# Linear attention and a multiplicative FFN on one core: a bfloat16 lead in the Gram sums, tiled features for batch 0 and for the second query block, and a new order of steps

## The chip, the cores and the metric

One core of one Trainium2 chip runs the whole program. The time is that of one execution on the device, in microseconds (us); of several runs the median is taken. The engines are TensorE (PE for its products, PEld for its weight loads), VectorE (DVE), ScalarE (ACT), GpSimd (POOL), and SyncE (SP), which issues most of the DMAs. Each engine works through its own instructions in a fixed order and waits for others only where data or a buffer makes it.

## The reference

```python
def phi(x):                                  # S1, S2: (8, 32)
    a = np.einsum('rd,bhsd->bhsr', S1, x)
    b = np.einsum('rd,bhsd->bhsr', S2, x)
    return np.einsum('bhsi,bhsj->bhsij', a, b).reshape(*x.shape[:-1], r * r)
q_p, k_p = (phi(q), phi(k))                  # q, k, v: (4, 4, 1088, 32)
kv = np.einsum('bhsf,bhsd->bhfd', k_p, v)
z = np.sum(k_p, axis=2)
num = np.einsum('bhsf,bhfd->bhsd', q_p, kv)
den = np.einsum('bhsf,bhf->bhs', q_p, z)[..., None] + 1e-06
attn_out = num / den
x = attn_out.transpose(0, 2, 1, 3).reshape(4352, 128)
a = x @ w1                                   # (128, 1024)
b = x @ w2
out = ((a * b) @ w3) @ w_out                 # (1024, 1024), (1024, 128)
```

Inputs are float64 and are handed over as raw 64-bit words; the output is float32. The denominator can come near zero, so its path is computed with split numbers (a coarse part on a grid, and a rest) so that the products of the coarse parts are exact.

## The kernel before

The program is written as named steps (`@step("...")` in `make_steps`). A string `ORDER` lists them; the steps are issued in that order, and every engine's instructions, and the DMAs among themselves, are chained in it. Nothing reorders them afterwards. `SLOTS` says for every tile which buffer of its kind it takes, in the order of allocation: `b` are the eight PSUM banks, `l`, `m`, `s`, `x`, `raw` are SBUF buffers of several sizes (`x` holds k, v and q of a batch). `POOL` and `ACTS` name the steps that run on GpSimd and ScalarE instead of VectorE (`on(name)`). A step can wait because its inputs aren't there or because the buffer that it takes is still read.

**Per batch b, keys and values.** `k{b}.load` brings 1024 rows of each head, `k{b}.loadr` the last 64. `k{b}.max` takes the largest absolute value, `k{b}.g` makes the grid (k_g), `lead` rounds k to it (on ACT in two activations, on DVE or POOL in one operation), `rest` is k minus lead; both lie in one float32 tile `kk`. `k{b}.gram0` to `gram4` (L607) sum, for each of 9 chunks and 4 heads, lead^T·[lead, rest] and rest^T·k: one product with 64 columns and one with 32 for each chunk and head, all float32, which run as two passes each. `Gm, Gt, Ga, Gb, T0, T1, Ta, Tb, Ts, N0, N1, Na, Nb, Nr` (`k_end`) make out of the Gram matrix and of S1, S2 (steps `s.*`) the matrix that gives the denominator; its results go to RC and AR (and RS, Rh for batch 0). The features of k are made in `kv(b)`: `tr`/`kT` turn k (through PE for batches 0 and 1, by DVE from `kh` for 2 and 3), `ab` multiplies by S, `kp0`, `kp1` form the 64 features, `kv0` to `kv3`, `kvr` sum features times v, and `kvm/kzt/kz` (batch 0) or `kvc/kqt/kq` lay the result out as weights. For batch 0, `ab0`, `ab1` (L650) are full-height products with kT as weights, copied out by ACT (`abc`); for the other batches `ab` (L675) works in 64x32 tiles and DVE turns the result (`abt`, L693). The last 64 rows of two batches go together (`kr0`, `kr1`).

**Queries.** q of a batch arrives with rows spread over heads. Block 0 (`q0`, 512 columns, kind "A") and block 1 (`q1`, 512 columns, kind "L") of batch 0 are done by `q_part`; batches 1 to 3 come as one block of 1024 each (`q2`, `q4`, `q6`), and the four last pieces of 64 rows as `qr`; these by `q_wide`. The steps of a block: `tr` turns it, `max`, `l2`, `l1` (ACT) and `rm` split it, `A*` and `C*` are the products with S and with the denominator's matrix, `sm, st, sh, sl, sc` split the results, `al, p01, p2, p12, dn, de, rc` give the reciprocal of the denominator, `bs` scales, `phi` forms the features, `pt/pc` (through PE and ACT, in `q_part`) or `pT` (by DVE, in `q_wide`) turn them, `x` multiplies by kv, and `xT` brings the result to the tile that the FFN reads. In `q_wide` the products work in 32x32 or 64x32 tiles, 16 or 8 side by side. In block 0 the scaling comes after x: `xs` multiplies by rc (DVE, L1206), `xt` turns it back (PE), `xT` copies (ACT).

**FFN.** Groups g0 to g7 have 512 tokens each and gr 256. For each group and each c of 8: `a` (L1453) and `b` (L1463) are products of 128x512, `c` copies a to SBUF (ACT), `m` multiplies (DVE, L1469), and `o` (L1476) adds the product with w3o to the group's sum in a bank. w3o = w3·w_out is made in 8 folds `f0` to `f7` (L479), each after its part of w3 has been converted from 64-bit words (`w{n}.c`, `w{n}.m` on ACT, `w{n}.j` on DVE, `w{n}.a0/a1` on POOL) and turned (`f.t`, DVE, L473). `oT` turns the sum (DVE) and `st` stores it (four DMAs on SP). g0 and g1 need q0 and q1, g2 and g3 need q2, and so on. g0 and g1 have 32 products a and b together, all in front of the first results of q2 unless the order puts some behind.

**Start.** Until the first `a`, PE's gaps are filled by products of zeros (`warm*`, L222). `c.act` is a copy of one element on ACT, whose only effect is that the table of activation functions is loaded there.

Of the kernel before, what the change touches and what calls it, by code (L numbers as in the profile page):

```python
# [24 lines left out]
        "s": "q1 s_t2 s_hla ay_A s_bs s_al kvc", "x": "k v qh"}  # L25
# [4 lines left out]
        "012345670123467012641234670513062571430516723512603215302725010760415320623547260134572614"  # L30
        "251376342057632057360276302162517325463712456142074372642354632462347562257341657163405264"
        "527053627367057653067434706730710014071506016364160573405671056454165341346354154112642167"
        "12047635102",
    "k_g": "0101",
    "l": "0123456789abc01246537804912cba076412583907a28bc67503914273a02145c0872195b6a34c8",
    "m": 
        "0123456789abcdefghijklmnopqrstuv3402158ab67cjefmil3hts8vc9dunb075c3hbnarkg7t4j38bv16euil9m"
        "oqs2htpe8u7oldnmt0qbjrchon294v5agd69s80onpvektuf387gbpkemd04lgntehs409vqodv9rsquh28rsft321"
        "gkcr",
    "q_m": "011010",  # L40
    "raw": "01210120120120120",
    "s": "0123456712054631027564013",
    "x": "012100120221",
}

WARM = [16, 10, 6] + [4] * 2 + [2] * 8 + [1] * 16
# [8 lines left out]
    k0.Nf k0.Nh k0.Nl k0.kp1 k0.rest0 k1.kp1 k2.kp0 k2.kp1 k2.rest0 k3.kp0 k3.rest0 q0.p01 q0.p12 q0.p2  # L55
    q0.scy q1.p12 q1.phi q2.bs q2.p2 q2.phi0 q2.phi1 q4.al q4.bs q4.p01 q4.p12 q4.phi0 q4.phi1 q4.sc
    q6.al q6.phi0 q6.phi1 qr.al qr.p12 s.blk s.blkh s.low s.rest s.sum
""".split())

ACTS = set("k0.lead1 k1.lead0 k2.lead0 s.lead".split())  # L60
# [15 lines left out]
g0.2a g0.3a q1.al q1.p01 q1.scy g0.2b q1.p2 g0.2c g0.1ac g0.3c w3.load k1.Gb v2.zero w1.a0 g0.5a g0.1ab q2.tr g0.7a
warm23 g0.6a g0.5c s.RC g0.7c g0.2m g0.1bb g0.1ba warm9 q1.p12 g0.0aa k2.rest0 w1.a1 g0.6c k1.T0 k1.T1 k2.gram0
k2.gram1 k2.gram2 k2.gram3 k2.gram4 q1.dn kr1.abc q2.max q1.de k1.Ta q1.rc w2.c k1.Tb k1.Ts q1.bs q2.l2 g0.0ac g0.1bc
k1.ab k1.N0 w3.c g0.1am q1.phi k1.N1 g0.4b g0.4a g0.1bm k1.abt k2.Gm k1.Na q2.l1 w3.m k2.Gt q1.pt1 q1.pt0 k0.Nr s.AR
q1.pc0 q1.pc1 g0.4c g0.7b g0.5b k1.Nb k1.Nr k2.Ga k1.kp0 k2.Gb q1.x q2.rm q2.C0 w3.j q1.xT w2.m w3.a0 w3.a1 v1.zero  # L80
q1.restT g0.5m q2.C1 q2.A0 g0.7m g0.4m q2.At q2.Ct g0.0ab g0.0am q2.sm g1.4a v1.load v1.loadr w2.j q2.st g1.0a g1.7a
g0.0bb k1.kp1 g1.6a g0.0ba g0.6b w4.load kh2.load g1.5a g1.4c g1.7c g1.6c q2.sh q2.sl q2.sc k1.kv0 k1.kv2 k1.kv3
q2.p01 k2.T0 k2.T1 k2.Ta q2.al k1.kv1 g1.5c g0.0bc k1.kvr k0.kqt k2.Tb g0.0bm g0.6m q2.p2 k2.kT0 k1.kvc w4.c w2.a0
q2.p12 q2.dn q2.de w2.a1 q2.rc g1.4b w5.load g1.1a q2.bs w4.m g1.6b g1.7b w5.m g1.7m f0.t q2.phi0 k3.zero g1.1b g1.2a
g1.5b w5.c q2.phi1 k0.kq q2.load k3.load g1.4m g1.0c g1.1c g1.1m g1.2c g1.5m g1.2b k2.kT1 k1.kqt f0.m k1.kq q2.pT0
kr1.kp w6.load f0.o q2.pT1 q2.restT g1.3a g1.3b g1.3c k2.Ts w4.j g1.3m q4.tr q2.x k2.N0 k2.N1 g0.3b q2.xT0 q2.xT1 w6.c
w6.m w9.load g0.3m g2.0a g3.6a w5.j g3.1a q4.max g3.6c g2.0c w5.a0 g2.1a g3.4a g3.3a g2.5a g3.1c g2.1c q4.l2 w5.a1
g2.1b w6.j g1.6m f2.t g2.7a w9.c g3.3c f2.m g1.0b w9.m g2.7c k2.Na w9.j k2.Nb g2.3a k3.loadr w4.a0 g3.0a f2.o g3.4c
q4.l1 g2.5c g2.3c g2.5b k2.Nr g3.0c w4.a1 g1.2m k2.ab g1.0m k3.max q4.rm q4.C0 w8.load w6.a0 q4.C1 q4.A0 k2.abt g2.5m
f1.t q4.At q4.Ct w8.m g2.4a g2.2a k2.kp1 w9.a0 w9.a1 w6.a1 f1.m g3.1b g2.6a g2.4b g3.5a f1.o w8.c g2.6c f6.t q4.sm  # L90
g3.1m q3.load w7.load q4.st g2.1m q4.sh w8.j w7.m w7.c g2.2c f3.t w8.a0 kh3.load k2.kp0 g1.0o v2.loadr g1.1o f6.m
g2.6b w7.j g0.0o g0.1o g0.2o k3.g k3.lead0 f6.o f3.m w7.a0 w7.a1 w8.a1 k3.kT0 f4.t q4.sl g2.4c f3.o q4.sc q4.al g2.6m
g1.6o g0.6o g1.3o g3.5c g2.2b g2.2m g2.7b g3.3b g3.2a g3.2c v2.load w10.load g2.7m f5.t g2.4m q3.restT f4.m k3.rest0
w10.c f5.m g3.4b q4.p01 q4.p2 w10.m q4.p12 q4.dn w10.j q4.de q4.rc q4.bs qr.max k2.kv0 k2.kv3 k2.kv1 k2.kv2 k2.kvr
q4.phi0 k3.gram0 k3.gram1 k3.gram2 q6.tr q6.max f5.o k3.gram3 k3.gram4 f4.o k2.kvc k2.kqt g3.6b w10.a0 k3.kT1 g3.4m
k3.Gm g1.4o k2.kq q6.l2 qr.l2 w10.a1 f7.t g2.3b g1.5o g2.0b g1.2o v3.zero k3.Gt g3.6m k3.Ga g2.0m g2.3m qr.l1 f7.m
g0.3o g0.5o g0.4o f7.o q6.l1 g3.3m k3.Gb q4.pT0 warm12 k3.T0 k3.T1 q4.phi1 q4.pT1 q6.rm q4.x k3.Ta k3.Tb k3.N0 k3.Ts
k3.N1 warm17 g1.7o k3.Na q4.xT1 g5.2a q4.xT0 k3.ab g1.oT k3.Nr k3.Nb q6.C0 k3.abt q6.C1 q6.A0 q6.Ct g0.7o v3.loadr
v3.load g1.st g4.4a q6.At g4.4b g2.0o q6.sm q6.st k3.kp0 g0.oT q6.sh k3.kp1 q6.sl g4.4c g2.4o g4.6a g4.6b g5.2c g4.6c
# [23 lines left out]
def make_steps(ctx, tc, q, k, v, S1, S2, moe_w1, moe_w2, moe_w3, moe_w_out, out):  # L123
# [3 lines left out]
    r = S1.shape[0]  # L127
# [430 lines left out]
    def k_split(b):  # L558
# [1015 lines left out]
```

## Time and profile before

| what | us |
|---|---|
| runs of the kernel | 250.39, 250.38, 249.95; median 250.38 |
| the profiled execution: time / span of its instructions | 250.19 / 248.4 |
| first product of the FFN (a_ps) | 28.77 |
| q2.x, q4.x, q6.x begin | 65.55, 123.01, 158.07 |
| last product (gr.o) ends | 245.17 |
| PE / DVE / ACT / POOL busy | 243.9 / 159.7 / 97.1 / 78.7 |

All times within the profile are from the start of the span. The profile's parts are: busy time of each engine; the span in 40 slices (about 6.2 us each), where a digit is the busy share in tenths; the chain of work that ended last; the groups of instructions by line, with mean duration, and with the idle time of the engine ahead of them and what ended it; and, from the trace, the instructions of an engine in order of time (start, duration, line, operation, tiles, a count where equal ones follow on each other, and in brackets how long the engine had been idle and what released it). Matmuls overlap, so the time of a run of products is read from start to start, not from the sum of durations. A float32 product shows as two instructions. The granted clock is 1.00 in every stretch.

### The profile page before, as it was taken

How to read it: one execution, taken by the hardware profiler on the slowest of the kernel's cores; microseconds unless marked ns; L12 is line 12 of the kernel's file. 1: busy time of each engine (PE TensorE's matmuls, PEld its weight loads, DVE VectorE, ACT ScalarE, POOL GpSimd, SP SyncE). 2: the span in 40 equal slices, each digit the busy share in tenths (PEclk: the TensorE clock that was granted, in tenths of full speed). 3: DMA queues.
4: the chain of work that ended last, by engine and by line, in shares of the span. 5: the costliest groups of instructions: out<-in, count | busy, mean ns of one | idle time of the engine just before them, and what ended most of it. 6: DMA issues, size and time to landing. Idle time of an engine off the chain costs nothing.

```text
span 248.4 us, 5734 instructions
## 1 busy us (share of the span) xinstructions
PE 243.9 (98%) x2375; PEld 139.2 (56%) x2375; DVE 159.7 (64%) x337; ACT 97.1 (39%) x178; POOL 78.7 (32%) x104
## 2 busy tenths in 40 slices
PE   8999999999999999999999999999999999999996
PEld 6889756464645556485644454444444445564455
DVE  4988999989988898887969483504256315142410
ACT  4578978458488271153213103422023221411000
POOL 5446693709473639769030005000000000000000
DMA  6889824887799307503020000002000000001563
GB/s 190 246 214 278 262 62 124 213 190 227 173 226 236 83 7 219 118 3 92 3 42 3 0 4 0 3 1 42 3 0 0 0 3 0 0 0 22 89 101 66
DMA packets 31130, 22.01 MB, mean 89 GB/s; under 512 B 21248, under 2 KB 25600, under 8 KB 30976
## 3 DMA queue, kind: packets, MB, share of 16 engines
q1 hardware_dynamic: 30416, 21.05, 34.8%
q10 hardware_dynamic: 688, 0.59, 0.7%
q8 instruction: 19, 0.31, 0.6%
q14 instruction: 7, 0.06, 0.1%
HBM read 19.40 MB, written 2.23 MB: 87 GB/s over the span
## 4 chain that ended last, share of the span: by engine, by line
PE 88%; DMA 4%; SPq 2%; DVE 2%; issue 1%; POOL 1%; ACT 0%; POOLq 0%; DVEq 0%
PE b_ps L1463 24%; PE a_ps L1453 24%; PE ps_o L1476 22%; PE ps_w3o L479 6%; DMA k<-in_k_dram 4%; PE ps_x L1412 2%; PE ps_ac L1299 2%; PE ps_or L1483 1%; PE ps_g L607 1%; PE ps_kv L717 1%; SPq L395 1%; DVE k_m L181 1%; PE ps_ab L675 1%; PE idle_ps L222 1%; POOL kk L599 0%
## 5 line engine op out<-in xcount | busy, mean ns | idle before, releaser
L1469 DVE TENSOR_TENSOR ab<-ffa,b_ps 128x512 f32<-128x512 f32 (+1 forms) x74 | 44.8, 633 | 44.3 <-PE b_ps L1463 33.5
L1458 ACT COPY ffa<-a_ps 128x512 f32<-128x512 f32 (+1 forms) x74 | 38.7, 558 | 87.0 <-PE a_ps L1453 78.9
L1463 PE MATMUL b_ps<-xT,w 128*128 128x512 f32 (+1 forms) x148 | 67.2, 561 | 0.0
L1453 PE MATMUL a_ps<-xT,w 128*128 128x512 f32 (+1 forms) x148 | 66.5, 560 | 0.0
L1476 PE MATMUL ps_o<-ab,w3o 128*128 128x512 f32 x128 | 60.7, 594 | 0.0
L1453 PEld LDWEIGHTS a_ps<-xT,w 128*128 128x128 f32 x148 | 27.5, 190 | 30.8 <-issue 24.0
L1463 PEld LDWEIGHTS b_ps<-xT,w 128*128 128x128 f32 x148 | 27.1, 190 | 27.0 <-issue 20.8
L1476 PEld LDWEIGHTS ps_o<-ab,w3o 128*128 128x128 f32 x128 | 23.9, 190 | 25.3 <-issue 23.7
L443 POOL TENSOR_TENSOR w3c<-cv_c,cv_m 128x512 int32<-128x512 int32 x16 | 21.1, 1349 | 13.1 <-DVE cv_c L432 13.1
L1492 DVE STREAM_TRANSPOSE oT<-ps_o 128x512 f32<-128x512 f32 x8 | 5.7, 715 | 22.9 <-PE ps_o L1476 22.9
L479 PEld LDWEIGHTS ps_w3o<-wo,w3T 128*128 128x128 f32 x128 | 15.3, 192 | 2.9 <-issue 2.2
L1394 POOL TENSOR_TENSOR ph<-s_al,s_bs 128x1024 f32<-128x1024 f32 x6 | 11.7, 1954 | 12.0 <-DVE s_bs L1384 11.8
L479 PE MATMUL ps_w3o<-wo,w3T 128*128 128x128 f32 x128 | 15.4, 275 | 0.0
L625 POOL TENSOR_TENSOR kp<-kabt 128x1024 f32<-128x1024 f32 x4 | 8.2, 2062 | 16.6 <-DVE kabt L693 16.6
L230 ACT ACTIVATE cv_c<-raw 128x1024 f32<-128x1024 f32 x11 | 12.8, 1164 | 0.6 <-issue 0.6
L222 PE MATMUL idle_ps<-zeros 128*128 128x256 bf16 x72 | 12.0, 313 | 1.0 <-DVE zeros L194 1.0
L418 ACT ACTIVATE cv_m<-raw 128x1024 int32<-128x1024 uint32 x11 | 12.8, 1172 | 0.0
L473 DVE STREAM_TRANSPOSE w3T<-w3c 128x1024 f32<-128x1024 f32 x8 | 9.9, 1240 | 3.9 <-POOL w3c L443 2.8
L222 PEld LDWEIGHTS <-zeros 128*128 128x128 bf16 x72 | 7.8, 112 | 3.6 <-DVE zeros L194 1.0
L1365 POOL TENSOR_TENSOR s_pr<-s_pr 128x256 f32<-128x256 f32 (+1 forms) x2 | 1.1, 526 | 25.3 <-DVE s_pr L1361 25.3
L483 ACT COPY w3o<-ps_w3o 128x128 f32<-128x128 f32 x8 | 2.0, 267 | 17.5 <-PE ps_w3o L479 17.5
L1402 DVE STREAM_TRANSPOSE pT<-ph 128x1024 f32<-128x1024 f32 (+1 forms) x7 | 7.9, 1147 | 0.0
(245 smaller groups left out, 292.4 us busy)
## 6 DMA issues: line engine op xcount, KB each, us to landing
raw<-in_moe_w_dram SPq DMA_DIRECT2D x32, 256.0 KB, 5.0
qh<-in_q_dram SPq DMA_DIRECT2D x4, 544.0 KB, 6.2
out_dram<-oT SPq DMA_DIRECT2D x33, 64.0 KB, 2.0
raw<-in_moe_w_dram SPq DMA_DIRECT2D x4, 512.0 KB, 7.6
k<-in_k_dram SPq DMA_DIRECT2D x3, 512.0 KB, 6.4
v<-in_v_dram SPq DMA_DIRECT2D x2, 512.0 KB, 4.4
raw<-in_moe_w_out_dram SPq DMA_DIRECT2D x1, 1024.0 KB, 8.7
kh<-in_k_dram SPq DMA_DIRECT2D x8, 128.0 KB, 2.5
```

The costliest lines, as they stand in the source:

```text
L222: pe.matmul(t, zeros, bview(zeros, [[0, 2], [1, 128]]), start=True, stop=True)
L230: act.activation(dst, hi.bitcast(F32), ACT.Prelu, scale=2.0 ** -112, alpha=-2.0 ** 32)
L418: act.mul(x["m"], words(0).bitcast(U32), 2.0 ** -29)
L443: pool.tensor_tensor(d, c, m, ALU.add)
L473: dve.transpose(w3T[ko].rearrange("p s (i r) -> p s i r", r=32), bview(w3c[ko], [[32, NC], [256, 4], [1, 32]]))
L479: pe.matmul(t["o"], w3T[ko][:, c], wo[:, c], start=c == 0, stop=c == NC - 1)
L1394: on(nm(f"phi{u}")).tensor_mul(x, bview(s["al"][:, u * g], [[r, g], [1, r], [0, r]]), bview(s["bs"][:, u * g], [[r, g], [0, r], [1, r]]))
L1453: pe.matmul(x["a"][:, :w], w_of(0, c), xT[g][:, c0:c0 + w], start=True, stop=True)
L1458: act.copy(x["s"][:, :w], x["a"][:, :w])
L1463: pe.matmul(x["b"][:, :w], w_of(1, c), xT[g][:, c0:c0 + w], start=True, stop=True)
L1469: dve.tensor_mul(ab_sb[g, c][:, c0:c0 + w], x["s"][:, :w], x["b"][:, :w])
L1476: pe.matmul(o_ps[g], w3o[:, c], ab_sb[g, c], start=c == 0, stop=c == NC - 1)
```

## The change

The Gram sums of batches 1 to 3: the lead is written in bfloat16 (into the first half of kk), the products lead^T·lead are bfloat16 with 32 columns (`gramH`); then `plus` replaces k by k + lead, and rest^T·(k + lead) is summed in float32 with 32 columns (`gram0`, `gram1`); `Gb` adds half of that sum and half of its transpose (`Gy`). Batch 0 keeps the float32 products, but has three grids of its own: heads 0 and 1, heads 2 and 3, and the last rows of all. Batch 0's features go the way of batch 1's (tiles, `abt`). Block 1 of the queries goes through `q_wide` (512 columns) instead of `q_part`. In block 0, x is now computed with kz as weights, so that it comes out turned; the reciprocal is spread by an ACT copy (`rb`), turned by PE (`rT`) and multiplied in by DVE (`xT`). `POOL` and `ACTS` name other steps, the warm products have other counts, `SLOTS` and `ORDER` are new from end to end.

```diff
-    k0.Nf k0.Nh k0.Nl k0.kp1 k0.rest0 k1.kp1 k2.kp0 k2.kp1 k2.rest0 k3.kp0 k3.rest0 q0.p01 q0.p12 q0.p2
-    q0.scy q1.p12 q1.phi q2.bs q2.p2 q2.phi0 q2.phi1 q4.al q4.bs q4.p01 q4.p12 q4.phi0 q4.phi1 q4.sc
-    q6.al q6.phi0 q6.phi1 qr.al qr.p12 s.blk s.blkh s.low s.rest s.sum
+    k0.Nf k0.Nh k0.Nl k0.Nr k0.Ts k0.rest0 k0.rest1 k0.rest2 k1.Nr k1.kp0 k1.kp1 k1.rest0 k2.kp0
+    k2.rest0 k3.Nr k3.Ts k3.kp0 k3.kp1 k3.plus k3.rest0 q0.al q0.p01 q0.p12 q0.p2 q0.phi1 q0.sca q0.scy
+    q1.al q1.p01 q1.p12 q1.p2 q1.phi0 q2.al q2.bs q2.p12 q2.p2 q2.phi0 q2.phi1 q2.sc q4.bs q4.p01
+    q4.phi0 q4.phi1 q4.sc q6.al q6.phi0 q6.sc qr.al qr.p01 qr.p12 qr.p2 qr.phi0 s.AR s.KS s.Pp s.blk
+    s.blkh s.low s.sum
-ACTS = set("k0.lead1 k1.lead0 k2.lead0 s.lead".split())
+ACTS = set("k0.lead0 k0.lead1 k0.lead2 k1.lead0 k2.lead0".split())
 ORDER
-s.load c.mask k0.zero c.zeros k0.load0 k0.loadr c.ident warm24 warm22 warm18 warm0 k0.load1 q0.load warm21 c.act
-s.words s.four k0.max0 s.pair k0.max1 k0.max2 k2.zero k0.tr1 k0.g s.lead warm3 warm1 warm7 s.low k0.lead0 k0.lead1
+c.zeros k0.zero k0.load0 c.mask s.load k0.load1 s.words c.ident k0.max0 warm0 warm1 k0.tr1 k0.g0 k0.loadr s.pair
+k0.max1 s.four s.lead s.low k0.lead0 q0.load k0.g1 k0.tr0 s.sum k0.max2 k0.lead1 s.rest k1.zero kr0.load k0.g2 warm2
+s.T s.tc s.P k0.rest0 warm3 s.R k0.kT1 k1.loadr q1.tr kr0.tr k0.rest1 k0.lead2 k1.load s.zero s.Pc warm4 k0.gram0
...
+k2.rest0 q3.restT q6.tr w6.a1 g2.0m f1.m g2.1c k2.ab q4.C0 q4.A0 f3.t q4.C1 f1.o k3.gramH k3.kT0 k3.plus q4.At k3.gram0
...
+qr.p01 g3.2o g2.4o qr.p2 qr.p12 qr.dn q6.bs c.act q6.phi0 q6.phi1 g4.4b g3.4o g2.7o g4.3m q6.pT0 q6.pT1 g3.5o q6.x
...
+gr.7c gr.2o1 g5.1o g5.7o gr.0o0 gr.2o0 g5.oT gr.5o1 gr.6b gr.7m g6.st gr.6m gr.1o0 gr.3o0 gr.4o0 g7.st gr.6o0 gr.6o1
+gr.7o1 gr.5o0 gr.7o0 gr.oT0 gr.oT1 g5.st gr.st1 gr.st0
```
```diff
 def k_split(b):
+        parts = ((0, 2, 0, NJ), (2, H, 0, NJ), (0, H, NJ, NK))
...
+        def lead_of(x):
+            t = bview(x, [[1, H * NK * D // 2]]).bitcast(BF16)
+            return t.rearrange("p (h j d) -> p h j d", h=H, j=NK)
...
+        @step(f"k{b}.plus")
+        def _():
+            on(f"k{b}.plus").tensor_add(k_sb[b], k_sb[b], k_lead[b])
 def gram(b):
+        if b > 0:
+            @step(f"k{b}.gramH")
+            def _():
+                a["g"] = ps("kvz", [128, 2 * D], "ps_g")
+                for j in range(NK):
+                    for h in range(H):
+                        prod(h, k_lead[b][:, h, j], k_lead[b][:, h, j], a["g"][:, :D], j == 0, j == NK - 1)
+            for u in range(2):
+                @step(f"k{b}.gram{u}")
+                def _(u=u):
+                    for j in range(*((0, 5), (5, NK))[u]):
+                        for h in range(H):
+                            prod(h, kk[b][:, 1, h, j], k_sb[b][:, h, j], a["g"][:, D:], False, j == NK - 1)
+            return
 def k_end(b):
+            dve.scalar_tensor_tensor(a["Gb"], a["g"][:, D:], 0.5, a["Gb"], ALU.mult, ALU.add)
+            dve.scalar_tensor_tensor(a["Gb"], a["Gy"], 0.5, a["Gb"], ALU.mult, ALU.add)
 def q_part (block 0)
+                    s["x", u] = o = ps("h", [128, 256], "ps_xt")
+                    for p in range(2):
+                        pe.matmul(o[64 * p:64 * (p + 1)], kz[b][:, 64 * p:64 * (p + 1)], s["pT"][:, p, part],
+                                  start=True, stop=True)
...
+                    dve.tensor_mul(x_dst()[:, part], x_dst()[:, part], s["rT", u])
     for g in range(8):
-        if g < 2:
-            q_part(g, b, half * 512, 512, "AL"[g])
+        if g < 1:
+            q_part(g, b, half * 512, 512, "A")
```

325 lines of the change are left out of this document (154 added, 171 removed).

## The prediction

> **What bounds the kernel now.** I read the busy line and the slices first, then the busy time in four stretches, then the rows where the stretches meet.
>
> ```profile
> PE 243.9 (98%) x2375; PEld 139.2 (56%) x2375; DVE 159.7 (64%) x337; ACT 97.1 (39%) x178; POOL 78.7 (32%) x104
> PE   8999999999999999999999999999999999999996
> DVE  4988999989988898887969483504256315142410
> ```
> ```profile
> 0.00:28.77 28.77, 26.69 (x586) 23.36 (x587) 23.00 (x70) 20.18 (x40) 14.46 (x52) 1.00 0.79 240
> 28.77:65.55 36.78, 36.78 (x449) 20.45 (x448) 35.15 (x86) 24.86 (x39) 22.98 (x22) 1.00 0.68 170
> 65.55:123.00 57.45, 57.45 (x600) 34.50 (x604) 50.26 (x76) 27.15 (x44) 33.90 (x25) 1.00 0.48 114
> 123.00:245.20 122.20, 122.20 (x748) 60.52 (x748) 50.97 (x108) 24.92 (x56) 7.39 (x6) 1.00 0.12 18
> ```
>
> Columns of the second view: stretch, then busy us of PE, PEld, DVE, ACT, POOL, then clock, DMA share, GB/s. PE looks full everywhere, but until 28.77 (first FFN product, a_ps) it is partly padded by `warm` products. From 28.77 on it does real work without a gap. DVE is nearly as full until 65.55 (35.15 of 36.78), then lighter. So there are two joints at which both run out together; they are where the tiled block of 1024 queries gets its output product `x`:
>
> ```profile
> 63.27 2.33 DVE L1402 STREAM_TRANSPOSE pT<-ph 128x1024 f32<-128x1024 f32 x2
> 65.55 0.81 PE L1412 MATMUL ps_x<-pT,kq 32*32 32x256 f32 x32
> ...
> 119.65 2.37 DVE L1402 STREAM_TRANSPOSE pT<-ph 128x1024 f32<-128x1024 f32 x2
> ```
> ```profile
> 31.16 0.86 PE b_ps L1463 x2
> ...
> 37.00 1.70 PE ps_g L607 x85
> ...
> 123.01 1.38 PE ps_x L1412 x58
> ...
> 241.60 3.57 PE ps_or L1483 x32
> ```
>
> DVE ends the pT of q2 at 65.60 and PE's q2.x starts at 65.55 (it takes the first half early): call this **A**. DVE ends q4's at 122.0 and q4.x starts at 123.0: **B**. Before A, PE has used up 30 of the 32 full FFN products that exist for the first two groups, so it can't run ahead of DVE there. From B to the last product (245.17) only PE counts. I therefore forecast A, then PE's work from A to B, then from B to the end; the rest (250.19 of the profiled execution less 245.17 = 5.0 us) stays: the stores of the last groups take about 0.5 us each on SP, and the 16 of g4, g6, g7, g5 now queue ahead of gr.st1 for 8 us, but their first data is there some 8 us before the end. The median of the runs, 250.38, is 0.19 above the profiled execution. From no change a measurement of this kernel tells about 0.2% (0.5 us).
>
> **Up to A: DVE.** Both kernels issue exactly 155 DVE instructions up to the second pT of q2. Added, by rows of the same shape: two k.plus (128x1152, 1.35 each) 2.7; pT of the second block 1.16; two more w.j conversions 1.38; two kabt transposes 0.78; six 128x128 transposes for q1's A and C (0.31 each) 1.86; two G_y and two more G_b operations 0.84; four small S steps from ACT and POOL 0.7. Sum 9.4. Removed: k0's lead and rest 0.66 + 0.78, k1's rest 1.35 (to POOL), one kT 0.69, one phi half 0.68, q1's and q2's corrections 0.86, three al 0.99, q0's sca 0.30, p01, p2 and p12 1.31, the P2 steps 0.64, KS and AR 0.9, half an ab 0.38. Sum 9.5. Net -0.1.
>
> Waits: `c.act` moves to the far end, so ACT's table load no longer runs beside the first transfers but behind them, with the first real activation:
>
> ```profile
> 1.74 1.28 ACT L215 ACT_TABLE_LOAD   x1 [1.74 <-issue]
> ...
> 3.71 0.26 ACT L230 ACTIVATE sk_c<-s_raw 8x64 f32<-8x64 f32 x1 [0.49 <-DMA s_raw<-in_S_dram]
> ```
>
> sk_c then starts at about 5.0. Behind it on ACT stand k0's two leads, and DVE's s.pair waits: with max0 and g0 done at 4.4, DVE idles till 5.2: +0.8. The Gram of k0 starts at about 9.7 (8.32 now), but DVE gets to it only at 11.75, behind two transposes, two q maxima and k1.max, so nothing more comes of that. DVE's wait of 0.76 for k2 at 24.46 goes: k2.load is issued some 2 us earlier and its maximum is asked for later. That is -0.76. The scaling of block 0 by a transposed reciprocal has as many DVE, PE and ACT steps as now; its chain (rc, copy, transpose, multiply) is as long as xs, xt, xT, and x now runs beside it: 0.
>
> POOL gets 13.6 us more before A (37.4 now): 2.64 for k1.rest0, 1.75 for k0's rests, 1.27 for half a phi, 1.27 for q2.sc, 0.62 for kpr, the rest small. Where both engines read at once the trace shows stretches:
>
> ```profile
> 36.20 0.99 DVE L1124 SCALAR_TENSOR_TENSOR s_rc<-s_d 128x16 f32<-128x16 f32 x1
> ...
> 94.04 1.90 DVE L587 TENSOR_TENSOR k_g<-k_m,grid 128x2 f32<-128x2 f32 x1
> ```
> ```profile
> 93.52 2.41 POOL L625 TENSOR_TENSOR kp<-kabt 128x1024 f32<-128x1024 f32 x1
> ```
>
> s_rc takes 0.17 elsewhere, k_g 0.15. Summed, DVE lost about 1.6 us in 37.4 us of POOL before A, and 5.1 in 33.9 between A and B: 0.04 to 0.15 per us of POOL. For 13.6 us that is 0.6 to 2.0; I take 0.8, the rate of the same stretch. A moves by -0.1 + 0.8 - 0.76 + 0.8 = **+0.7**, to 66.3.
>
> PE does not set A: its work from 28.77 loses q1's four-by-two transposes (0.88), a kqt (0.22), three warm products (0.33), 0.26 of x and 0.55 of Gram (below), and gets 1.5 FFN products more (at 0.858): 35.8 instead of 36.8 us. It can start at about 28.1, since DVE's work ahead of the first xT is 0.6 more and its waits some 0.4 more, but the new order begins with half products that need half of xT. So PE could be at A by 63.9. What PE saves before its first FFN product (C of q1, about 1.1; x of q0, about 1.4) only replaces warm-up time: 0.
>
> **A to B: PE.** Counting the products in both orders: 44.5 full FFN products instead of 43 (+1.29), k3's N0 and N1 now before B (+0.24), two warm products fewer (-0.2), and k3's Gram. That is 144 passes in 1.70 us now; its first 8 wide passes take 0.14 us, the next 7 narrow ones 0.06, so 17 and 8.5 ns a pass. Afterwards 72 narrow passes stay (0.6) and 36 bf16 products of 32 columns with their own weight load come: at least the narrow pass (8.5 ns, 0.31), at most the bf16 products of L976 (four in 0.10, 0.90). I take 15 ns, 0.54: the Gram saves 0.55, bounds 0.2 and 0.8. Sum **+0.8**.
> The Trainium skill, TensorEngine Tiling (Array Packing), section Instruction Overhead, speaks against a fourfold gain from bf16: a product carries some 60 cycles of its own, so that few columns cost as much as 60. By it the bf16 product costs what the narrow pass costs, the Gram saves 0.8, and the sum would be 248.6; by the trace's bounds it is 248.6 to 249.2.
> DVE's work grows by 4.0 there (a q.rm 1.1, a kp 1.13, T steps 0.85, a kT 0.62, p12 0.6, al 0.35, G_y 0.35, less two w.j): 54.3 of 58.2 us. It fits if its idle 7.2 us shrink to 4.
>
> **B to the end: PE.** 124 full products instead of 127 and N gone: **-2.8**. The new order puts 39 products between q4.x and q6.x (33 now), so q6 has more cover; 17 before qr.x cover its short chain.
>
> Sum: 250.19 + 0.7 + 0.8 - 2.8 = **248.9**.
>
> **Rivals.**
> *PE alone bounds* (DVE's waits close up, POOL does not disturb): A at 63.9, so -1.65 + 0.8 - 2.8 gives 246.5. For it: PE is full from 28.77. Against it: DVE's sum up to A is unchanged. 0.14.
> *POOL holds DVE up before A*: at 0.15 per us and with POOL's own steps stretched once (p01 of q0 took 1.78, the same shape 0.73 elsewhere), A moves by 0.7 + 1.2 + 0.4, and the time is 250.5, no change. 0.15. The Trainium skill, SBUF — State Buffer, section Who interferes with whom, gives this as a lock: a DVE instruction with two SBUF inputs and a GpSimd instruction exclude each other, for the whole instruction. The trace agrees at k_g: it ends at 95.94, the POOL kp at 95.93.
> *DVE becomes the bound between A and B, and the change is slower*: its idle time there is not slack but waits for POOL's w3c, PE's b and the k3 chain (k3.max, lead, then rest0 and plus on POOL, 2.64 each, before PE's k3.gram0 that stands in the middle of PE's queue). If all 7.2 us of waiting stay, A to B takes 61.5 instead of 58.2: 252.2. It decides from about 2.1 us kept beyond the forecast's 4. For it: DVE is 88% busy there now and gets 8% more. Against it: PE's FFN work lies in wait on every other step. 0.25.
> *The change does not do what it says*: the bf16 Gram costs as much as the f32 one. Only k3's share lies on the path: +0.55, 249.4, inside the forecast's band.
>
> **How the numbers follow.** Forecast 248.9 (247.7 to 249.7) 0.46; PE alone 246.5 0.14; POOL's hold 250.5 0.15, a third of it over 250.9; DVE bound 252.2 0.25, a fifth of it under 250.9. Faster 0.62 (the first two and a little of the third), same 0.13, slower 0.25. The range reaches from 246.2 to 252.0 and leaves out the upper half of the last case and a little of the second.
>
> **What would show it.** Right: sk_c at about 5.0 behind the table load; the Gram of k2 and k3 in 0.9 to 1.5 us; q2.x at 66.3 with DVE's pT just ahead; q4.x about 58 us later; last product at 243.9. Wrong: q2.x before 65 (PE or a shorter DVE queue bounds), or PE gaps before k3.gram0 or q4.x with DVE busy there.

## The result: 6 % slower, and the profile after

The changed kernel takes 265.17 us (median of 4 runs, 264.07 to 267.8), the kernel before 250.22 beside it: 1.061 times, 95% interval 1.053 to 1.070. Ratios, here and below, leave out executions that took over 1.5 % longer than the fastest of their kernel; medians keep them. The forecast was 248.9 with a range up to 252.0. The profiled execution of after took 265.82, with a span of 264.0. Its busy line and slices:

```profile
PE 249.4 (94%) x2374; PEld 135.3 (51%) x2374; DVE 170.0 (64%) x335; ACT 96.7 (37%) x179; POOL 100.6 (38%) x126
PE   8969798898899997999999999999999999999995
DVE  3959899899999998999557913571363013461212
PEclk9977979999799999999999999999999999999999
```

PE was full from its first FFN product in the kernel before; now it has gaps in the first sixteen of the 40 slices, and among these the granted clock falls too. DVE is busy for 170.0 us instead of 159.7, with two instructions fewer. Where the time went is told by three stretches, up to joint A (q2.x begins), from A to joint B (q4.x begins) and from B to the last product. First the kernel before, then after; columns: stretch, busy us (and instructions) of PE, PEld, DVE, ACT, POOL, clock, DMA share, GB/s:

```profile
0.00:65.55 65.55, 63.47 (x1034) 43.81 (x1034) 58.14 (x155) 45.03 (x78) 37.44 (x73) 1.00 0.73 200
65.55:122.94 57.39, 57.39 (x591) 34.45 (x590) 50.20 (x76) 27.15 (x44) 33.90 (x25) 1.00 0.48 114
122.94:245.20 122.26, 122.26 (x750) 60.58 (x748) 51.03 (x108) 24.92 (x56) 7.39 (x6) 1.00 0.12 18
```
```profile
0.00:79.94 79.94, 70.30 (x1080) 42.24 (x1080) 69.38 (x154) 47.84 (x81) 54.86 (x91) 0.91 0.68 178
79.94:141.31 61.37, 59.57 (x570) 34.22 (x573) 52.62 (x86) 24.39 (x42) 33.81 (x25) 1.00 0.39 89
141.31:260.90 119.59, 119.50 (x738) 58.80 (x736) 48.05 (x97) 24.22 (x55) 11.97 (x11) 1.00 0.10 18
```

A is 14.4 us late, A to B 4.0 longer, B to the end 2.7 shorter. Up to A, DVE issues 154 instructions instead of 155, yet is busy for 11.2 us more, and idle for 10.6 instead of 7.4. POOL is busy for 17.4 more. The same instructions have become longer. Seven of them, from DVE's timeline of after (start, duration, engine, line, operation):

```profile
22.45 3.20 DVE L663 TENSOR_TENSOR kp<-kabt 128x1024 f32<-128x1024 f32 x1
31.96 1.24 DVE L1149 SCALAR_TENSOR_TENSOR s_rc<-s_d 128x16 f32<-128x16 f32 x1
35.58 0.89 DVE L602 TENSOR_TENSOR k_g<-k_m,grid 128x2 f32<-128x2 f32 x1
39.53 2.30 DVE L170 SCALAR_TENSOR_TENSOR s_t<-s_g,ay_A 128x256 f32<-128x256 f32 x1
55.22 2.31 DVE L1301 SCALAR_TENSOR_TENSOR q<-q,qT 128x1024 f32<-128x1024 bf16 x1
61.69 2.09 DVE L170 SCALAR_TENSOR_TENSOR s_t<-s_g,ay_A 128x512 f32<-128x512 f32 x1
65.60 1.12 DVE L839 SCALAR_TENSOR_TENSOR G_b<-G_y,G_b 128x32 f32<-128x32 f32 x1
```

Undisturbed, they take some 1.2, 0.16, 0.12, 0.37, 1.2, 0.65 and 0.18 us, by the shortest instruction of the same operation and shape in the traces. What GpSimd did meanwhile, from its timeline:

```profile
21.17 3.40 POOL L617 TENSOR_TENSOR kk<-k,kk 128x1152 f32<-128x1152 f32 x1 [0.31 <-DMA raw<-in_moe_w_dram]
...
39.18 2.38 POOL L617 TENSOR_TENSOR kk<-k,kk 128x1152 f32<-128x1152 f32 x1 [1.47 <-ACT kk L178]
...
55.18 3.52 POOL L445 TENSOR_TENSOR w3c<-cv_c,cv_m 128x512 int32<-128x512 int32 x2
...
61.28 1.96 POOL L663 TENSOR_TENSOR kp<-kabt 128x1024 f32<-128x1024 f32 x1
```

The kp of 22.45 starts while k1's rest runs, which ends at 24.57, and ends 1.1 us behind it, about its own undisturbed time; s_t of 39.53 ends at 41.83, k2's rest at 41.56. So two steps on GpSimd hold up two DVE instructions by 2 us each. k1's rest was moved there by the change; k2's was there in the kernel before too (33.27 to 35.91), but beside transposes, reductions and a product that reads PSUM, and held up none of them. Counted over the stretch up to A, 18 DVE instructions that read SBUF alone and run beside GpSimd are over 0.1 us longer than their shortest, by 14.2 us together; in the kernel before there are 7, by 2.0 us.

The waits on DVE ahead of A: 2.25 us at 17.42 for q0.C0, which stands behind kr1.tr on PE; 0.86 for sk_c; 1.58 for GpSimd, 1.42 of it before the sums that read its p12. The first of these I had not foreseen. PE's row and DVE's, from their timelines:

```profile
16.03 0.33 PE L782 MATMUL ps_krt<-ident,kr 128*128 128x128 f32 x1 [1.94 <-issue]
...
17.42 0.29 DVE L1037 TENSOR_REDUCE s_ga<-ps_ac 128x16 f32<-128x128 f32 x1 [2.25 <-PE ps_ac L992]
```

"issue" says that PE waited 1.94 us for nothing that the profile shows.

### The profile page after: what moved, and what is told of

It reads as the page before. It is cut to its first block, busy times and chain, and to the rows that moved or that the text cites. A ratio compares the mean times of both kernels' runs of the same rounds, so it can differ in the third digit from the quotient of the medians.

```text
span 264.0 us, 5765 instructions
## 1 busy us (share of the span) xinstructions
PE 249.4 (94%) x2374; PEld 135.3 (51%) x2374; DVE 170.0 (64%) x335; ACT 96.7 (37%) x179; POOL 100.6 (38%) x126
## 4 chain that ended last, share of the span: by engine, by line
PE 76%; DVE 17%; issue 3%; POOL 2%; ACT 1%; DVEq 0%; POOLq 0%
PE b_ps L1487 20%; PE ps_o L1500 20%; PE a_ps L1477 18%; PE ps_w3o L481 4%; PE idle_ps L224 3%; DVE kp L663 2%; PE ps_x L1436 2%; DVE s_t L170 2%; DVE ab L1493 1%; PE ps_or L1507 1%; PE ps_ac L1323 1%; DVE q L1301 1%; PE ps_kv L732 1%; PE ps_ab L693 1%; DVE k_m L183 1%
## 5 line engine op out<-in xcount | busy, mean ns | idle before, releaser
L1493 DVE TENSOR_TENSOR ab<-ffa,b_ps 128x512 f32<-128x512 f32 (+1 forms) x74 | 45.4, 631 | 52.1 <-PE b_ps L1487 41.6
L1477 PE MATMUL a_ps<-xT,w 128*128 128x512 f32 (+1 forms) x148 | 67.4, 576 | 0.1
L1477 PEld LDWEIGHTS a_ps<-xT,w 128*128 128x128 f32 x148 | 28.3, 196 | 30.1 <-issue 22.6
L1487 PEld LDWEIGHTS b_ps<-xT,w 128*128 128x128 f32 x148 | 27.3, 191 | 28.5 <-issue 23.1
L445 POOL TENSOR_TENSOR w3c<-cv_c,cv_m 128x512 int32<-128x512 int32 x16 | 23.4, 1487 | 11.4 <-PE ps_o L1500 5.8
L1418 POOL TENSOR_TENSOR ph<-s_al,s_bs 128x1024 f32<-128x1024 f32 (+1 forms) x7 | 13.8, 1979 | 19.7 <-DVE s_bs L1408 19.6
L224 PE MATMUL idle_ps<-zeros 128*128 128x256 bf16 x67 | 12.8, 345 | 1.1 <-DVE zeros L196 1.0
L1447 ACT COPY xT<-ps_x 128x256 f32<-128x256 f32 (+2 forms) x20 | 5.1, 343 | 15.9 <-PE ps_x L1436 8.1
L1375 POOL TENSOR_TENSOR s_al<-s_hl 128x256 f32<-128x256 f32 (+2 forms) x4 | 4.2, 1055 | 17.4 <-DVE s_hl L1370 17.2
L663 POOL TENSOR_TENSOR kp<-kabt 128x1024 f32<-128x1024 f32 x5 | 10.2, 2042 | 1.6 <-DVE kabt L711 1.6
L1426 DVE STREAM_TRANSPOSE pT<-ph 128x1024 f32<-128x1024 f32 (+1 forms) x8 | 9.1, 1161 | 1.4 <-POOL ph L1418 1.4
```

What stands on the lines that cost most here:

```text
L224: pe.matmul(t, zeros, bview(zeros, [[0, 2], [1, 128]]), start=True, stop=True)
L445: pool.tensor_tensor(d, c, m, ALU.add)
L663: eng.tensor_mul(dst, bview(av, [list(av.ap[1]), list(av.ap[2]), [0, r]]), bview(bv, [list(bv.ap[1]), [0, r], list(bv.ap[2])]))
L1418: on(nm(f"phi{u}")).tensor_mul(x, bview(s["al"][:, u * g], [[r, g], [1, r], [0, r]]), bview(s["bs"][:, u * g], [[r, g], [0, r], [1, r]]))
L1477: pe.matmul(x["a"][:, :w], w_of(0, c), xT[g][:, c0:c0 + w], start=True, stop=True)
L1487: pe.matmul(x["b"][:, :w], w_of(1, c), xT[g][:, c0:c0 + w], start=True, stop=True)
```

## Experiments

Thirteen kernels in five steps. Where a step is moved, the slot letters that it takes move with it; that part of the diffs is left out. In the table, A is the start of q2.x in the profiled execution, DVE its busy time up to there, idle the rest; the ratio is to the kernel before as it ran beside each (medians 249.9 to 250.63), with its 95% interval.

| kernel | A | DVE busy | idle | median us | ratio |
|---|---|---|---|---|---|
| before | 65.55 | 58.14 | 7.41 | 250.22 | 1 |
| after | 79.94 | 69.38 | 10.56 | 265.17 | 1.061 (1.053 to 1.070) |
| tr_late | 77.64 | 68.89 | 8.75 | 263.89 | 1.051 (1.045 to 1.056) |
| warm_fill | 79.67 | 69.33 | 10.34 | 264.02 | 1.054 (1.051 to 1.058) |
| rest_dve | 76.89 | 67.81 | 9.08 | 262.53 | 1.045 (1.040 to 1.051) |
| before_pool | 73.05 | 54.35 | 18.70 | 257.40 | 1.026 (1.021 to 1.030) |
| pool_old | 83.23 | 69.80 | 13.43 | 266.93 | 1.068 (1.065 to 1.070) |
| pool_old_tr | 81.27 | 69.32 | 11.95 | 266.86 | 1.069 (1.061 to 1.077) |
| gram_alone | 71.41 | 62.22 | 9.19 | 258.72 | 1.033 (1.028 to 1.038) |
| mix | 76.48 | 67.63 | 8.85 | 262.75 | 1.051 (1.043 to 1.058) |
| mix_gram_old | 79.48 | 63.47 | 16.01 | 267.26 | 1.070 (1.065 to 1.076) |
| dummy_pool | 69.91 | 63.40 | 6.51 | 254.64 | 1.017 (1.015 to 1.019) |
| w0_late | 82.13 | 68.78 | 13.35 | 264.58 | 1.056 (1.052 to 1.059) |
| rest_cut | 77.01 | 65.26 | 11.75 | 263.12 | 1.052 (1.049 to 1.055) |

The variants of the changed kernel scatter by 0.4 to 2 % from run to run, the kernel before and dummy_pool by 0.6 % or less; differences of 1 us between two of them are not read as differences of time, only their traces are.

### Step one: four single edits

**tr_late**
```diff
-... q1.l1 warm5 k0.T1 kr1.tr v0.load s.KS q0.C0 ... k0.Na k0.Nh k1.tr1 ...
+... q1.l1 warm5 k0.T1 v0.load s.KS q0.C0 ... k0.Na k0.Nh kr1.tr k1.tr1 ...
```


> The changed kernel with one step moved: the transposes of k's last rows (kr1.tr) stand on PE after k0's ab instead of ahead of q0's C. Theory P (GpSimd's added work stretches VectorE's instructions: summed, 11.2 of the 14.4 us that joint A came later): only the 2.25 us wait of VectorE behind that step goes, so q2.x moves from 79.9 to 77 to 78 and the time from 265.2 to 262 to 263.5. Rival C (TensorE's empty 2 us and the fall of the granted clock behind it cost most): the clock stays at 1.00 from 16 to 24, and 6 us or more come back: below 260.

A comes 2.3 us earlier, within theory P's bounds: the wait at q0.C0 shrinks from 2.25 to 0.58 us, and little else changes. The clock stays at 1.00 from 16 to 24, and the median is 1.3 us lower (263.89; P said 262 to 263.5), not rival C's 5 or more. But the moved step is hardly what did it. PE's stop at this place lasted 0.47 us here instead of 1.94 (what it is comes in step three). In w0_late (step four) kr1.tr stands as in the changed kernel, the stop lasts 0.51 us, and DVE waits as little. First tr_late, then w0_late:

```profile
15.85 0.29 DVE L1037 TENSOR_REDUCE s_ga<-ps_ac 128x16 f32<-128x128 f32 x1 [0.58 <-PE ps_ac L992]
```
```profile
15.84 0.29 DVE L1037 TENSOR_REDUCE s_ga<-ps_ac 128x16 f32<-128x128 f32 x1 [0.62 <-PE ps_ac L992]
```

**warm_fill**
```diff
-WARM = [3, 16, 14, 2, 6, 1, 2, 1, 5, 11, 6]
+WARM = [3, 16, 14, 2, 6, 18, 2, 1, 5, 11, 6]
-... q1.l1 warm5 k0.T1 kr1.tr ...
+... q1.l1 k0.T1 warm5 kr1.tr ...
```


> The changed kernel with 17 more warm products on PE just ahead of kr1.tr, where it waits 2 us for its DMA: the wait of VectorE stays as it is, only TensorE is kept busy. Expected in both theories: the granted clock no longer falls to 0.50 between 17 and 23. Theory P: VectorE sets the pace there, so at most 1 us comes back: 264 to 265.5. Rival C (the lower clock itself costs): 3 us or more come back: below 262.

From 17 to 23 the clock is 1.00, in after 0.50. A moves by 0.3 us. It is not a clean test of the price: in this run the clock fell to 0.50 earlier, from 10.8 to 14.2, and DVE waited 1.04 us there for k0's Gram sums. From the end of the wait at q0.C0 (18.17, in after 17.42) to A it takes 61.5 us instead of 62.5. So the fall costs about 1 us by this pair of traces; the 3 us or more of rival C are out.

**rest_dve**
```diff
-    k0.rest0 k0.rest1 k0.rest2 k1.Nr k1.kp0 k1.kp1 k1.rest0 k2.kp0 k2.rest0 ...
+    k0.rest0 k0.rest1 k0.rest2 k1.Nr k1.kp0 k1.kp1 k2.kp0 ...
```


> The changed kernel with k1's and k2's rest (a subtraction of 128x1152) on VectorE again instead of GpSimd. VectorE gets 2 x 1.35 = 2.7 us more of its own. Theory P: kp takes 1.22 us instead of 3.20, s_t of q1 0.4 instead of 2.30, GpSimd's al of q0 starts some 3 us earlier: q2.x 2 to 4 us earlier, 261 to 263. Rival (VectorE is bound by its own sum, overlap with GpSimd is incidental): 1 to 2.7 us slower, 266 to 268.

A comes 3.05 us earlier, although DVE has 2.7 us more of its own: its busy time falls by 1.6. But 0.7 of the 3.05 are there ahead of the first rest already: PE's stop lasts 1.33 us instead of 1.94, and DVE goes on at 16.71 instead of 17.42.

**before_pool**
```diff
+    k0.rest1 k1.rest0 k1.kp0 q0.al q0.sca q0.phi1 q1.al q1.p01 q1.p2 q2.al q2.p12 q2.sc
```


> The kernel before in its own order, with twelve steps before joint A put on GpSimd as the changed kernel has them (rests of k0 and k1, one kp, half a phi, al, p01, p2, p12 and sc of q0, q1, q2): some 7 us of instructions leave VectorE, some 13 us come to GpSimd. Theory P: VectorE's remaining instructions are stretched by 5 us or more and wait for GpSimd's chain, so that q2.x comes 3 to 10 us later than 65.55: 253 to 260. Rival (VectorE's own sum sets joint A): q2.x earlier, 246 to 249.

7 us slower, in the undisturbed order of before. But not by more busy time: DVE is busy for 3.8 us less up to A, and idle for 11.3 more, 7.1 of it in waits for GpSimd's chain sc, al, p01, p12. The time came out as theory P said, the way to it only half: work moved to GpSimd comes back as a stretch or as a wait.

### Step two: everything back, and the Gram alone

**pool_old**
```diff
-    k0.Nr k0.Ts k0.rest1 k0.rest2 k1.Nr k1.kp0 k1.rest0 q0.al q0.phi1 q0.sca q1.al q1.p01 q1.p2
-    q2.al q2.p12 q2.sc s.AR s.KS s.Pp
+    s.rest
```


> The changed kernel in its own order, with every step ahead of joint A on the engine that the kernel before gave it: 19 steps go from GpSimd to VectorE (k0's Nr, Ts, two rests, k1's Nr, kp0 and rest, al, phi1 and sca of q0, al, p01, p2 of q1, al, p12, sc of q2, AR, KS, Pp of S), s.rest goes the other way. By durations of the undisturbed rows VectorE gets about 8 us more of its own. Theory P (stretches and waits from GpSimd): VectorE's stretch before A falls from 17 to 5 to 9 us and its waits for GpSimd from 1.6 to about 0, so that q2.x comes at 76 to 79 and the time is 261 to 264. Rival (VectorE's own sum decides): q2.x at 85 or later, time 270 or more.

A miss for theory P: A comes 3.3 us later, not earlier, and the time lies between the two expectations. The 8 us of instructions came to DVE and the stretches fell by nearly as much (busy +0.4), but the idle time grew by 2.9: the new order is laid out for the steps on GpSimd, and DVE now stands 3 us before ps_rt (block 0's reciprocals, turned on PE). So the stretches alone are not the cause. As I read it, the change has 9.4 us of new vector work ahead of A, and neither engine has room for it: with the old engines DVE has some 8 us more of its own, undisturbed, than in the kernel before.

**pool_old_tr** (pool_old, kr1.tr as in tr_late, and `c.act` behind `k0.load1`)

> As pool_old, and besides kr1.tr behind k0's ab on PE, and the small copy that makes ScalarE load its table ahead of the first transfers, as in the kernel before. If the causes add up: 2.2 us (the wait for kr1) and 0.9 us (sk_c at 3.7 instead of 5.0) better than pool_old, 258 to 261; q2.x at 73 to 76. If what is left is the order itself, it stays 8 us or more over the kernel before (250.4). Rival (the waits only move on to the next step): within 1 us of pool_old.

A comes 2.0 us earlier than in pool_old; the time is the same (266.86), as the rival had it. It stays 17 us behind the kernel before.

**gram_alone** (the kernel before, with k_split, gram, Gy and Gb of the changed one)
```diff
-... k0.kzt k1.rest0 q0.C1t ... q0.x1 k1.gram0 k1.gram1 k1.gram2 k1.gram3 k2.g q0.rc w0.a0 k1.gram4 ...
+... k0.kzt k1.rest0 k1.plus q0.C1t ... q0.x1 k1.gramH k1.gram0 k2.g q0.rc w0.a0 k1.gram1 ...
...
```


> The kernel before with the first part of the change alone: the Gram sums of k1 to k3 from a bfloat16 lead and a symmetrised rest, the sum k + lead on VectorE for k1 and k2, on GpSimd for k3; order and everything else as before. VectorE gets 2 x (1.35 + 0.4) = 3.5 us ahead of joint A, PE loses 0.2 to 0.8 us a block. If VectorE sets joint A, as forecast: q2.x 2.5 to 3.5 later, 252.5 to 254. Rival (PE sets it, and the cheaper Gram counts): 248.5 to 250.

8.8 us slower, more than either theory said. DVE is busy for 4.1 us more up to A, as forecast, but idle for 1.8 more, and after A PE waits some 2 us more for k3's later chain (1.2 us idle from A to B, 0.7 behind B). The Gram products themselves are cheaper: for k1 144 passes with 1.89 us busy before, 108 with 1.08 here (1.32 in the changed kernel). That saving is on an engine with nothing waiting for it; the price is on the one that bounds.

### Step three: the Gram taken out of the changed kernel

**gram_old**
```diff
-            k_lead[b] = lead_of(kk[b])
+            k_lead[b] = kk[b][:, 0]
-            on(f"k{b}.plus").tensor_add(k_sb[b], k_sb[b], k_lead[b])
+            pass
...
+                            prod(h, kk[b][:, 0, h, j], kk[b][:, :, h, j], a["g"], j == 0, False)
...
```


> The changed kernel with its Gram sums of k1 to k3 as in the kernel before (float32 lead, 36 wide and 36 narrow products, no k + lead, no transposed rest); order and engines else as changed. Theory Q (revised: joint A comes when VectorE and GpSimd together are through their vector work; a step moved from one to the other saves nothing, only work taken away does): VectorE loses 2 x 1.36 for the sums and 2 x 0.4 for the transposes ahead of A, 3.5 us, and perhaps a stretch: q2.x at 75 to 77, time 260 to 262. Rival (only order and engines count, the Gram is neutral): within 1 us of 265.

**mix** (tr_late, rest_dve and `c.act` behind `k0.load1` together)

> The changed kernel with three repairs at once: kr1.tr behind k0's ab, the rests of k1 and k2 on VectorE, ScalarE's table load ahead of the first transfers. Theory Q with causes that add up: 2.3 (kr1.tr), 3.0 (rests, as measured alone) and 0.8: q2.x at 73.5 to 75, time 259 to 260.5. Rival (they hide one another): not below 261.5.

**mix_gram_old** (mix, with the edit of gram_old)

> As mix, and the Gram sums as in the kernel before. Theory Q: 3.5 us or a little more below mix, 254.5 to 257, q2.x at 69 to 71; what is left over the kernel before (4 to 7 us) is the second query block in tiles, block 0 and the order. Rival: no more than 1 us below mix.

Theory Q falls. mix is no faster than rest_dve (A 0.4 us earlier), and without the new Gram both kernels become slower, by 6 and 4.5 us (gram_old, not in the table: 270.95 us, 1.081, 1.075 to 1.087; its profiled execution took 273.69, and only its records of PE and of the DMA are read here). In mix_gram_old DVE is busy for 4.2 us less, as Q said, but idle for 7.2 more: it waits 7.1 us for ps_rt, and that waits on PE, in the middle of k1's Gram sum:

```profile
32.73 0.27 PE L629 MATMUL ps_g<-k,kk 128*32 128x32 f32 x2 [5.42 <-issue]
```

Again PE stands for nothing that the profile shows. Counting what PE has done up to each such stop tells what it is. The busy time from the start to the end of the stop, with the number of PE and PEld records in brackets, of two stops in after (1.94 and 0.90 us) and then of mix_gram_old's:

```profile
0.00:16.00 16.00, 12.97 (x221) 10.14 (x221) 10.51 (x35) 11.61 (x22) 10.10 (x50) 1.00 0.75 214
0.00:33.45 33.45, 27.92 (x604) 20.51 (x604) 24.82 (x61) 19.25 (x36) 23.09 (x65) 0.90 0.70 197
```
```profile
0.00:32.70 32.70, 22.95 (x604) 18.05 (x605) 22.96 (x63) 19.37 (x36) 17.08 (x62) 0.98 0.81 224
```

442 records, 1208, 1209. 1208 - 442 is 766, three times 256 less two; the next stop of after, 1.09 us at 46.96 in k2's Gram sum, comes at record 1458, 250 later (a few records are missing in a trace). The first stop is at record 442 in after, rest_dve, pool_old, gram_old, w0_late and rest_cut, where kr1.tr stands there; at 443 in tr_late, mix and mix_gram_old, where kr1.tr was moved away and q0.C0 stands there; and at 439 in the kernel before, in k0's ab (0.61 us at 13.77). The instruction does not matter, its number does. The page's list of DMA queues, of after, says what comes in such portions:

```profile
q8 instruction: 18, 0.29, 0.5%
```

18 packets of 16 KB for PE's 4748 records: one for every 256 or so. PE's code arrives in blocks, and a run of short products uses one up before the next is there. The times of these packets, in the trace's records of the DMA, confirm it. In after, four of them end at 14.59, 32.00, 45.55 and 103.51, and PE goes on at 16.03, 33.51, 46.96 and 104.91. In the fifteen traces PE stops 31 times for over 0.4 us with "issue" as the reason, and each time it goes on 1.2 to 1.6 us after the end of such a packet. The Trainium skill, Runtime: NRT & Kernel Launch, section Instruction fetch mechanics, states blocks of 16 KiB, 256 instructions, fetched while the block before runs, and calls the cost of a boundary mostly hidden. The trace agrees on the size, and on mostly: behind 14 of the 18 packets of after PE does not stop for over 0.4 us. Where it does, the stops last 0.45 to 6.3 us (the longest in gram_old). That mix_gram_old loses on balance is thus the larger stop rather than the Gram: at record 1209 mix stops for 1.58 us, mix_gram_old, which gets there inside a run of short products with eight loads of FFN weights issued from 23.1 to 27.3, for 5.42. The difference, 3.8 us, is most of the 4.5.

### Step four: the two mechanisms by themselves

**dummy_pool** (in the kernel before)
```diff
+    def spare(name, times):
+        @step(name)
+        def _():
+            x = bview(ident, [[0, 2], [1, 128]])
+            for _ in range(times):
+                pool.tensor_mul(k_pair[0].rearrange("p h d -> p (h d)").bitcast(BF16).rearrange("p (g c) -> p g c", g=2), x, x)
+
+    for i, n in enumerate((3, 2, 2, 5, 7)):
+        spare(f"d.{i}", n)
...
+(order) s.blkh d.0 ... k0.Nl d.1 ... q0.p12 d.2 ... q1.phi d.3 ... k1.kp1 d.4
```


> The kernel before, unchanged but for 19 additional GpSimd multiplications (128x256, 0.73 us each, 14 us in all, about what the change added ahead of joint A) whose result nobody reads, put where GpSimd is idle ahead of A. VectorE, PE and ScalarE have exactly the work and the order of before. Theory P (a GpSimd instruction holds up VectorE's instructions with two SBUF inputs): VectorE's stretch ahead of A grows from 5.5 us by 3 us or more, and the time to 252 to 256. Rival (the price of the prediction, 0.04 to 0.15 us per us of GpSimd): 0.6 to 2 us, 250.8 to 252. Second rival (GpSimd's work costs only when somebody waits for its result): no change, 250 to 250.6.

Theory P. Nobody waits for these results, VectorE's work and order are those of before, and its busy time up to A rises by 5.3 us:

```profile
0.00:69.91 69.91, 63.89 (x1034) 43.48 (x1034) 63.40 (x154) 45.01 (x78) 53.62 (x92) 1.00 0.68 188
```

A is 4.4 us late and the time 4.3 us longer (1.7 %, with the narrowest interval of the study): 0.3 us per us of GpSimd work, against the 0.06 that I took.

**w0_late**
```diff
-... k1.tr0 w0.load k0.Gb ... q0.sha w0.m k0.Nb ... v0.loadr q0.smy w1.load ... q0.p01 w0.c ...
+... k1.tr0 k0.Gb ... q0.sha k0.Nb ... v0.loadr w0.load q0.smy w1.load ... q0.p01 w0.m w0.c ...
```


> The changed kernel with the load of w0 moved from ahead of v0's load to just ahead of w1's, and its first conversion on ScalarE moved to its second. Theory F (new): PE's stop of 1.94 us at 13.95 is no wait for kr1 but for the next block of 256 instructions, which the DMA queue of instructions has to bring beside the data (442 matmul and weight-load records stand ahead of the stop in the changed kernel, 443 in the one with kr1.tr moved away, 439 in the kernel before, which stops there 0.61). With less data in the queues at 12 to 14 us the stop should shrink to 1.2 us or less, at the same record 442. Rival (it waits for kr1's rows): the stop ends when kr1 lands, whatever the number of records, and may go away altogether. Time 263 to 265 if VectorE's wait shrinks with it; more if w0 then comes too late.

The DMA share up to the end of the stop falls from 0.75 to 0.46, and the stop to 0.51 us, at the same record (221 and 221):

```profile
14.65 0.33 PE L782 MATMUL ps_krt<-ident,kr 128*128 128x128 f32 x1 [0.51 <-issue]
...
34.11 0.64 PE L1323 MATMUL ps_ac<-q,RC 32*32 32x128 f32 x6 [3.77 <-issue]
```

The second row is the price: the loads that were moved now stand beside the later block, whose stop grows from 0.90 to 3.77. Both fit theory F, that PE's code shares the DMA engines with the data and the stop goes where the traffic goes, and both lie outside what the kernels with the same order of products and w0's load in its old place show there (1.33 to 2.25 us at record 442; 0.90 to 1.94 at record 1208). That kr1 is not what PE waits for is shown, by the records and the packets. The part of the traffic is not fully shown: in tr_late the first stop lasts 0.47 us with a share of 0.71 and no load moved. No time is won.

### Step five: GpSimd's work taken away

**rest_cut**
```diff
-            on(f"k{b}.rest0").tensor_sub(kk[b][:, 1], k_sb[b], k_lead[b])
+            c = slice(0, 1 if b < 3 else NK)
+            on(f"k{b}.rest0").tensor_sub(kk[b][:, 1, :, c], k_sb[b][:, :, c], k_lead[b][:, :, c])
```


> The changed kernel in which GpSimd computes the rests of k1 and k2 for 128 of 1152 columns only (the other columns keep ScalarE's intermediate sum, so this part of the Gram sums is left wrong): some 4.5 us of GpSimd go, VectorE keeps exactly its work and order. Theory P: kp takes 1.2 us instead of 3.2, s_t of q1 0.4 instead of 2.3, and what queued behind them on GpSimd comes earlier: q2.x 4 to 6 us earlier than 79.94, time 259.5 to 261.5. Rival (stretches elsewhere take their place, since the other GpSimd steps then fall on other instructions of VectorE): less than 2.5 us, 263 or more.

```profile
0.00:77.01 77.01, 67.70 (x1080) 41.36 (x1080) 65.26 (x154) 47.95 (x81) 49.89 (x91) 0.93 0.71 185
```

GpSimd is busy for 5.0 us less, and DVE, with the same instructions, for 4.1 less: both long stretches are gone and none as long takes their place. Of these 4.1 us, 1.2 are given back in idle time (PE's second code stop grows from 0.90 to 1.94), and A comes 2.9 earlier. A lies between the two expectations, the time, 263.12, just in the rival's; the mechanism is P's, the rest is F's.

## Why the prediction was wrong

Joint A was forecast 0.7 us later than before; it came 14.4 later. The sum against what was measured, by its own steps:

- **DVE's work, net -0.1: right.** 154 instructions instead of 155; busy +11.2, and the stretches (each instruction against the shortest of its shape) make up 11 to 12 us, so the work itself changed by less than 1.
- **Table load, +0.8: right.** The load stands at 3.72, sk_c at 5.01 as said, and DVE's wait is 0.86. **k2's wait, -0.76: right**, waits for DMA fall by 1.0.
- **POOL's hold, "I take 0.8, the rate of the same stretch": this is the step that failed.** The amount of work was right: POOL is busy for 17.4 us more, and some 5 to 6 of these are more stretches of its own (k1's rest takes 3.40 against 2.38, s_loy 1.56 against 0.45), so about 12 against my 13.6. The price was not: 0.8 forecast, some 12 us measured (DVE's instructions beside GpSimd, 14.2 us too long in after, 2.0 before). I divided the stretch seen before by all of POOL's time before, 0.04 to 0.15 us per us, as if it were a rate (and the rate of the same stretch, 1.6 in 37.4, would have made 0.6, not 0.8). It is an event that happens or does not, and depends on which DVE instruction starts under which POOL instruction; the order before put few of the sensitive ones there, 7 against 18. With POOL's time added blindly (dummy_pool) the price is 0.3, in the changed order 11.2 / 12 = 0.9. The rival "POOL holds DVE up" had the mechanism and gave it 1.6 us and a chance of 0.15, from the same wrong rate.
- **"A step removed from DVE" as a gain: wrong in kind.** Of the 9.5 us that I counted as removed, most went to GpSimd. before_pool shows what such a removal brings in an order with room: DVE 3.8 us less busy, 11.3 us more idle.
- **Missing: PE's code blocks.** A stop of 1.94 us behind DVE's wait of 2.25 at 17.42, and one of 1.43 in k3's Gram sum at 104.91. The stop of 0.61 at 13.77 was in the trace of before, and the forecast has no term for it.
- **A to B, +0.8: measured +4.0.** The count of FFN products was right: those that start there are worth 89 records of full width instead of 86, +1.29. New are the code stop of 1.43, other idle time of 0.4, and q2.x, which started on its first half and takes 2.4 us instead of 1.6 to the next FFN product, while DVE still turns the second half (pT from 79.24, behind GpSimd's ph, to 80.49). The Gram saves 0.39 for k3, the one in this stretch, and 0.57 for k1, of 0.55 taken. Some 0.5 of the 4.0 us stay unexplained. PE is idle for only 1.8 of the 61.4 us and DVE busy for 52.6, so the rival "DVE becomes the bound" did not happen; that it gave nearly the same length, 61.5, is luck.
- **B to the end, -2.8: right** (-2.7).

Joint A was the place to look: I said that both engines run out there together, and then let the change fill the second vector engine as if it had been free.

What stays open: how much of the 14 us is the order itself. gram_alone costs 8.8 us in the old order, taking the Gram out costs 4.5 more in the new one; in both cases steps were put into an order that was laid out for other durations, and stops of PE's code moved with them. No variant of the changed kernel came nearer than 11 us to the kernel before, so none of the causes tried carries the loss alone. The cost of the second query block in tiles, and of block 0's new scaling, was not tried alone.

## What to carry to other kernels

A step moved from VectorE to GpSimd is not removed: list the VectorE instructions with two SBUF inputs that will run beside it, price them at the rest of the GpSimd instruction, and count what then waits for the slower engine; if VectorE bounds the stage, expect a loss. A saving on TensorE is worth nothing in a stage that another engine bounds, while its price there (here one addition of 1.36 us and a transpose a block) is paid in full. Where short products come in hundreds while loads are running, count PE's records: every 256th is a place where it may stop.

## What the runs showed of the hardware

- **Which VectorE instructions GpSimd holds.** In six kernels (before, after, tr_late, rest_dve, mix, dummy_pool; up to 125 us) I took the DVE instructions that start inside a GpSimd TENSOR_TENSOR with more than 0.2 us left beyond their own shortest time. Two inputs, both in SBUF: 69 of 71 are stretched by over 0.2 us, all 71 by 0.86 on average. Two inputs, one in PSUM: 0 of 127. Transposes and reductions: 0 of 136. TENSOR_SCALAR from SBUF: 9 of 9. The Trainium skill, SBUF — State Buffer, section Who interferes with whom, gives this rule: two inputs in SBUF contend with a GpSimd instruction that reads SBUF, one input does not, except in modes that use both ports, which it says tensor_scalar can enter; the one that issues first holds the other for the whole instruction. The trace agrees on each, and GpSimd is held as well (k1's rest 3.40 us against 2.38).
- **PE's code blocks**, as above: stops at record 442 plus multiples of 256, each over 1.2 to 1.6 us after a packet of code has ended; of 0.51 us with a DMA share of 0.46 up to there, 1.94 with 0.75 (but 0.47 with 0.71), 5.42 in a run of short products beside eight loads of weights. The scatter of up to 2 % of some variants of the changed kernel, against 0.6 % of the kernel before, would fit stops that depend on the traffic of the moment; no run tests that.
- **The granted clock** fell to 0.50 for 6.8 us (from 16.8) behind the stop of 1.94 us; in warm_fill, with 17 more products that nobody needs in its place, it was 1.00 there, but 0.50 from 10.8 to 14.2.
- **36 bfloat16 products of 32 columns** with their weight loads start within 0.25 to 0.36 us (24.80 to 25.10 for k1), 7 to 10 ns apiece, about as much as a narrow float32 pass (8.5 to 8.9): near the lower bound of the forecast (0.31).
